# A graph message-passing kernel: X ahead of the prefix sums while no batch is in the pipe, and the aggregate's zeros copied by DMA

## The chip, the core and the metric

The kernel runs on one core of a Trainium2 chip. Its engines are TensorE (PE; PEld is its weight loading), VectorE (DVE), ScalarE (ACT), GpSimd (POOL) and SyncE (SP), which issues most DMAs. Each engine takes its own instructions in program order and waits on semaphores for the others. The metric is the device time of one execution in microseconds. Before the change it is 8952.63 us (median of 3 runs, 8952.41 to 8958.04).

## What is computed

N = 12500 nodes with D = 64 features, E = 800000 edges with 16 attributes each; `src` and `dst` are random.

```python
N, D = x.shape
m_in = jnp.concatenate([x[src], x[dst], e_attr], axis=-1)
msg = _silu(m_in @ w_msg)
agg = _segment_sum(msg, dst, N)
return _silu(jnp.concatenate([x, agg], axis=-1) @ w_upd)
```

## The kernel before

**Two pipes in one loop.** The edges arrive unsorted. The first pipe bins them by destination into 128 buckets of `BK = 98` nodes, in a DRAM store `st` that holds tiles of 128 records for each bucket. The second pipe takes full tiles out of the store, computes the messages of their edges and adds them to the aggregate `ACC`, which lies in SBUF as 128 partitions x 128 buckets x 98 nodes. One call of `period()` moves both pipes on by one stage. `step()` (L852) calls it 782 times with a new step of `M = 8` columns of 128 edges each; a batch of the second pipe comes along whenever a group of tiles is ready. Further calls after the steps work off what is left.

**The binning pipe.** Its stages are methods of `Step`, and their order over the engines is that of the calls in `period()` (L708), written out by hand. In period k, for the new step h = k, the step before it z = k-1, and the one before that p = k-2:

- `onehot` of h (L387): ACT writes the one-hots `hf` of the bucket numbers, eight squares (L391) and one Relu (L392).
- `count` of z (L411): PE makes in the PSUM tile `z`, of which there is one, the place of each edge in its bucket: from `hf` (L418), the running sums `G` (L419) and the last of these (L421).
- `ranks` of z (L423): DVE reduces `z` to one rank an edge (L426).
- `sums` of h (L394): the running sums `G` over four columns at a time, one copy on ACT (L398) and, for the first 140 steps, three additions on DVE (two of L400, one of L402). The count of the following period reads them.
- `expand` of z (L428): DVE writes the records into the slots that the ranks name, the rows `X`: L435, L436 and four multiplications of L439. There are two buffers of `X`. The move of the following period reads them.
- `move` of p (L442): 16 matmuls of `hf` and `X` (L456; one instruction of the program's eight is two in the profile) gather the records by bucket in the PSUM tile `pl`; ACT copies it to `blk` (L461).
- `place` (L470): DVE advances the buckets' pointers (L474, L475). POOL scatters `blk` to the store one period later (L479).

Records are made of the edge attributes `ea`, loaded by SP for three steps at a time (L243) and copied by ACT (L272).

**The message pipe.** A group of tiles is formed over several periods (`fourth`, L527): pointers on DVE, then a work list, then SP loads the tiles, 16 a period at first, from the store into one of four buffers `RT` (L561), and DVE takes the node numbers out of them (`sidx`, L522). A group's batches then run through `gather` (POOL, L642), `onehot` (L652, L653), `transpose`, `product`, `message`, `reduce` and `add` (L703), one period apart: in `period()` the names q, t, a and r are the new batch and those of one, two and three periods before. The first group needs as many records as fill its tiles, so the first 26 periods (0 to 25) have no batch. Periods 34 to 38 get no new batch either; the last ones before them are still under way in 34 and 35.

**Tables.** Beside the first steps, `tables()` (L211) makes from the node features x the products with the two halves of w_msg, four bucket rows an iteration: PE transposes and multiplies (L193, L198), ACT copies (L194, L204, L205), SP stores one product to DRAM (`A_d`, L209) and loads x for a later iteration (L187). `BW`, on chip, keeps the other and gets 16 rows of w_msg by one DMA of 512 KB (L352). After each of the steps 0 to 3 come four iterations, after each later one a single one, up to step 21.

**Zeros.** `later()` (L345) is called after each step from step 1 on, behind the step's tables, while its list lasts. It zeroes the four buffers `RT` (1088 columns of 128 partitions each) and `ACC` in four pieces (3136 columns each), all by ACT (L347). Behind the first piece SP writes sentinel tiles to the store, behind the third it issues the DMA into `BW`. A group may load fewer tiles than `RT` holds; the rest of the buffer keeps what is there.

Of the kernel before, what the change touches and what calls it, by code (L numbers as in the profile page):

```python
# [6 lines left out]
AF = mybir.ActivationFunctionType  # L7
# [8 lines left out]
NBK = 128  # L16
BK = 98
D = 64
DE = 16
R = DE + 1  # L20
# [12 lines left out]
GT = NBG * BT  # L33
# [15 lines left out]
def mpnn_kernel(tc, x, e_attr, src, dst, w_msg, w_upd, out):  # L49
    nc = tc.nc  # L50
# [22 lines left out]
    with es:  # L73
# [68 lines left out]
        done0 = cp.tile([NBK, 1], F32, name="done0")  # L142
# [190 lines left out]
        RT = [lp.tile([P, GT, R], F32, name=f"rt{i}") for i in range(4)]  # L333
        ACC = lp.tile([2 * D, NBK, BK], F32, name="ACC")
        ACCf = ACC.rearrange("p b k -> p (b k)")
# [3 lines left out]
        nc.gpsimd.memset(sent[:, :, DE:R], (P - 1) / 256.0)  # L339
        nc.gpsimd.memset(done0, 0.0)  # L340

        ZP = NBK // 4
        zeros = [RT[i].rearrange("p a c -> p (a c)") for i in range(len(RT))] + [ACC[:, b:b + ZP, :].rearrange("p b k -> p (b k)") for b in range(0, NBK, ZP)]

        def later():  # L345
            z = zeros.pop(0)
            nc.scalar.activation(z, done0[0:z.shape[0], :].to_broadcast(z.shape), AF.Copy)  # L347
            if len(zeros) == 7:
                for k in range(P // SR):
                    nc.sync.dma_start(st_t[D0:D0 + DUM, k * SR * R:(k + 1) * SR * R], sent[0:DUM].rearrange("p a b -> p (a b)"))  # L350
            elif len(zeros) == 5:
                nc.sync.dma_start(BW[BK:KQ], w_msg[2 * D:2 * D + DE, None, :].to_broadcast([DE, NBK, D]))  # L352


# [353 lines left out]
        def period(step=None, batch=None, ptr_new=None):  # L708

            h, z, p, s = step, pipe["h"], pipe["z"], pipe["s"]  # L710
            q, t, a, r = batch, pipe["q"], pipe["t"], pipe["a"]
            forms = [g for g in work["forming"] if not g.ready()]
            e = None
            pipe.update(h=h, z=z, q=q, t=t, a=a)
            if q:
                q.gather(0, BT // 2)
            if s:
                s.scatter()
            if q:
                q.gather(BT // 2, BT)  # L720
            if h:
                h.onehot()
            if q:
                q.onehot()
            for g in forms:
                g.fourth()
            if z:
                z.count()
            if t:
                t.transpose(0)  # L730
                t.weights()
                t.transpose(1)
            if r:
                r.reduce()
            if z:
                z.ranks()
            if a:
                a.message()
            if r:
                r.add()  # L740
            if h:
                h.sums()
            if z:
                z.expand()
            if p:
                e = p.move(0)
            if t:
                t.product()
            if p:
                p.move(1)  # L750
            if e:
                e.place(ptr_new)
            for g in forms:
                g.middle()
                g.fifth()
            pipe["s"] = e
            return r
# [4 lines left out]
        class Draws:  # L762
# [34 lines left out]
            def take(d, u, units):  # L797
                for f, done in zip(d.free(u), d.done):
                    left = units
                    for b in range(NB):  # L800
                        n = min(f[b], left)
                        done[b] += n
                        left -= n
# [48 lines left out]
        def step():  # L852
            c = None
            if flow["ic"] < len(steps):
                c = next_step(flow["ic"])
                flow["ic"] += 1
            pn = None
            if pipe["z"] and pipe["z"].last:
                if flow["npl"] % 64 == 0:
                    flow["ptrs"] = sg.tile([NBK, 64], I32, name="ptrs")  # L860
                pn = flow["ptrs"][:, flow["npl"] % 64:flow["npl"] % 64 + 1]
                flow["npl"] += 1
            b = take()
            if size() and may_start() and draws.holds(state["u"], size() // state["u"]):
                draws.take(state["u"], size() // state["u"])
                g = stages[state["stage"]]
                start_group(state["u"], state["ptr"], size(), cap=g["cap"], bt=g["bt"])
            elif not size() and (not work["forming"] or work["forming"][-1].k >= 2):
                larger_from()
            if pipe["z"]:  # L870
                for i in pipe["z"].last.values():
                    draws.place(Chunk(i).m)
            period(c, b, pn)
# [4 lines left out]
        while flow["ic"] < len(steps) or pipe["h"] or pipe["z"]:  # L878
            step()
            for _ in range(4 if flow["ic"] < 5 else 1):  # L880
                next(tab, None)
            if zeros and flow["ic"] > 1:
                later()
        while zeros:
            later()
# [23 lines left out]
        while pipe["s"]:  # L909
            period(None, take())  # L910
# [21 lines left out]
        while work["used"] < large or (work["forming"] and work["forming"][-1].k < 2):  # L932
            b = take()
            if work["used"] < large and may_start():
                start_group(QU, ptrg)
            period(None, b)
            next(upd, None)
            next(upd, None)
# [61 lines left out]
        while work["used"] < whole or lasts or work["cur"] is not None or work["forming"]:  # L1000
            b = take()
# [47 lines left out]
        with tc.If(more > 0):  # L1049
# [4 lines left out]
            with tc.If(nover > 0):  # L1054
# [27 lines left out]
                with tc.For_i(0, nover, 1):  # L1082
# [36 lines left out]
                    def block(rs=None):  # L1119
                        for c in halves:  # L1120
                            c.expand(rs)
                            e = c.move()
                        return e


                    c = block()
# [4 lines left out]
                    with tc.For_i(0, rounds, 1):  # L1131
                        c = block(rs)
# [36 lines left out]
```

## Time and profile before

One profiled execution; the "mean" of a group in the profile is the mean duration of one instruction.

| what | value |
|---|---|
| median of 3 runs | 8952.63 us |
| profiled execution, time | 8968.66 us |
| profiled execution, span from first to last instruction | 8966.8 us |
| PE busy | 8230.5 us (92%) |
| DVE busy | 7221.8 us (81%) |
| POOL busy | 6615.6 us (74%) |
| ACT busy | 5079.7 us (57%) |
| mean granted TensorE clock | 0.940 |
| first period with a batch, sidx of its group | 225.37 us |

How to read the rows: in the timeline a row starts with its start and its length in us, then the engine, the line, the operation and the tiles written and read; "x16" merges sixteen such instructions that follow one another, and the brackets at the end hold the idle time of the engine before them and who ended it. "SPq" is the DMA issue on SP. In the table of stages the columns are the stretch, its length, the busy us of PE, PEld, DVE, ACT and POOL with the count of instructions, the granted clock, the share of time that the 16 DMA engines are busy, and GB/s. A row of a DMA queue has its packets, its MB and the time of its packets as a share of 16 engines' time. A busy engine can still be waiting for nothing but its own chain: the share of a stage tells only whether an engine is full.

### The profile page before, as it was taken

To read this page: it belongs to the slowest core of one execution; us is meant where nothing else is said; L and a number is where in the kernel's file an instruction comes from. 1 tells how busy PE (TensorE), PEld (TensorE's weight loads), DVE (VectorE), ACT (ScalarE), POOL (GpSimd) and SP (SyncE) were. 2 spreads that over 40 slices of the span, in tenths; PEclk is the share of its full clock that TensorE was granted. 3 is DMA by queue.
4 is the path that set the end of the run, shared out by engine and by line. 5 is a ranking of instruction groups with operands and counts; after the bars stand their busy time and mean duration, and the time that the engine had idled before them with its cause. 6 is when DMAs were issued, how large, how long until landed. Compare 5 with 4: busy or idle time off the path is not lost. (4 is left out here: it accounts for less than half of the span.)

```text
span 8966.8 us, 156158 instructions
## 1 busy us (share of the span) xinstructions
PE 8230.5 (92%) x49816; PEld 5882.3 (66%) x49816; DVE 7221.8 (81%) x15722; ACT 5079.7 (57%) x12601; POOL 6615.6 (74%) x6908
## 2 busy tenths in 40 slices
PE   8899999999999999999999999999999999999767
PEld 5677766666666666666666666666666666666656
DVE  7999998888888888888888888888888888887233
ACT  7666666555555555555555555555555555555222
POOL 1677777777777777777777777777777777777776
PEclk9999999999999999999999999999999999999566
DMA  3222222221222222222222221221222122221223
GB/s 67 56 60 61 61 62 57 52 55 51 56 53 54 53 55 55 52 57 52 55 52 56 56 53 51 55 58 50 57 52 55 52 56 56 52 57 49 59 48 51
DMA packets 660741, 493.05 MB, mean 55 GB/s; under 512 B 492743, under 2 KB 529671, under 8 KB 659911
## 3 DMA queue, kind: packets, MB, share of 16 engines
q0 software_dynamic: 238976, 349.72, 15.0%
q1 hardware_dynamic: 420615, 133.18, 6.9%
q8 instruction: 401, 6.57, 0.3%
q14 instruction: 429, 3.51, 0.1%
q10 hardware_dynamic: 320, 0.07, 0.0%
HBM read 330.05 MB, written 152.30 MB: 54 GB/s over the span
## 5 line engine op out<-in xcount | busy, mean ns | idle before, releaser
L642 POOL DMA_INDIRECT g<-A_d,sidx x6322 | 6036.2, 955 | 1949.3 <-issue 1511.9
L456 PE MATMUL pl<-X,hf 128*128 128x291 f32 (+5 forms) x12512 | 4273.7, 494 | 35.8 <-DVE LOST L474 35.8
L456 PEld LDWEIGHTS pl<-X,hf 128*128 128x128 f32 x12512 | 2398.5, 198 | 1374.1 <-issue 883.0
L439 DVE TENSOR_TENSOR X<-cb,rec 128x442 f32<-128x442 f32 (+5 forms) x3128 | 2647.7, 909 | 26.7
L391 ACT ACTIVATE hf<-iof,shi 128x128 f32<-128x128 f32 x6256 | 1914.0, 392 | 892.7 <-PE pl L456 892.6
L670 PEld LDWEIGHTS pre<-w,qt 114*128 114x128 f32 x10496 | 1334.3, 202 | 585.0 <-issue 568.5
L670 PE MATMUL pre<-w,qt 114*128 114x64 f32 x10496 | 1338.1, 284 | 256.9 <-DVE g L674 255.4
L674 DVE TENSOR_TENSOR g<-pre,g 128x512 f32<-128x512 f32 (+1 forms) x818 | 549.2, 671 | 1191.5 <-DMA g<-A_d,sidx 764.5
L675 ACT ACTIVATE g<-g 128x512 f32<-128x512 f32 (+1 forms) x818 | 503.0, 615 | 1742.6 <-DVE g L674 1740.7
L691 PE MATMUL ag<-q,g 128*64 128x98 f32 x12644 | 775.0, 264 | 248.2 <-DVE wl L546 133.6
L426 DVE TENSOR_REDUCE rank<-z 128x8 f32<-128x1024 f32 x782 | 950.3, 1215 | 53.6 <-PE z L421 27.0
L392 ACT ACTIVATE hf<-hf,ones 128x1024 f32<-128x1024 f32 x782 | 900.4, 1151 | 25.4
L664 ACT ACTIVATE qt<-tq 114x1024 f32<-114x1024 f32 (+1 forms) x818 | 799.0, 977 | 158.7 <-PE tq L661 157.4
L661 PE MATMUL tq<-ident,q 128*114 128x128 f32 x6322 | 873.2, 283 | 14.4 <-ACT nodes L194 12.7
L691 PEld LDWEIGHTS ag<-q,g 128*64 128x64 f32 x12644 | 613.5, 143 | 410.3 <-issue 211.9
L661 PEld LDWEIGHTS tq<-ident,q 128*114 128x114 f32 x6322 | 768.6, 140 | 137.4 <-ACT nodes L194 20.1
L479 POOL DMA_INDIRECT st<-blk,ptrs x567 | 572.8, 1010 | 342.2 <-issue 145.7
L461 ACT ACTIVATE blk<-pl 128x512 f32<-128x512 f32 (+1 forms) x568 | 324.2, 571 | 798.1 <-PE pl L456 643.9
L652 DVE TENSOR_TENSOR q<-cb,lo 128x784 f32<-128x784 f32 (+1 forms) x818 | 768.4, 939 | 2.2
L418 PE MATMUL z<-hf,w 128*128 128x512 bf16 x1564 | 619.7, 396 | 3.2 <-ACT hf L392 3.2
L703 DVE TENSOR_TENSOR ACC<-ag,ACC 64x98 f32 x1938 | 498.0, 257 | 107.7 <-PE ag L691 29.3
L419 PE MATMUL z<-G,onesb 128*128 128x384 bf16 x1564 | 512.0, 327 | 3.0 <-DVE G L400 2.9
(138 smaller groups left out, 5123.2 us busy)
## 6 DMA issues: line engine op xcount, KB each, us to landing
g<-A_d,sidx POOLq DMA_INDIRECT x6322
ea<-in_e_attr SPq DMA_DIRECT2D x260, 192.0 KB
rt<-st SPq DMA_DIRECT2D x1312, 34.0 KB
st<-blk,ptrs POOLq DMA_INDIRECT x567
rt<-st SPq DMA_DIRECT2D x434, 8.5 KB
nodes<-in_x SPq DMA_DIRECT2D x62, 98.0 KB
rt<-st SPq DMA_DIRECT2D x320, 17.0 KB
A_d<-nodes SPq DMA_DIRECT2D x32, 98.0 KB
```

What stands on the lines that cost most here:

```text
L391: nc.scalar.activation(c.hf[:, k, :], iof, AF.Square, bias=c.hi[:, k:k + 1])
L392: nc.scalar.activation(c.hf, c.hf, AF.Relu, bias=ones, scale=-1.0)
L418: nc.tensor.matmul(c.z[:, k:k + ZB, :], w1, hb[:, k:k + ZB, :], start=True, stop=False)
L426: nc.vector.tensor_reduce(out=c.rank, in_=c.z, axis=AX.X, op=OP.max)
L439: nc.vector.tensor_tensor(out=c.x[:, k:k + 2, 2:2 + n * R].rearrange("p k (s c) -> p k s c", c=R), in0=hit[:, k:k + 2, 0:n, None].to_broad ...
L456: nc.tensor.matmul(pl[:, 0:w], c.hf[:, k, :], c.x[:, k, 0:w], start=(n == (c.size - 1 if whole else 0)), stop=ends, skip_group_check=True)
L642: j = nc.gpsimd.indirect_dma_start(out=t.g[:, i, :], out_offset=None, in_=A_d, in_offset=bass.IndirectOffsetOnAxis(ap=t.grp.sidx[:, k:k + ...
L652: nc.vector.tensor_tensor(out=t.q[:, 0:n, 0:BK], in0=ioB[:, None, 0:BK].to_broadcast([P, n, BK]), in1=t.grp.lo[:, i0:i0 + n, None].to_broa ...
L661: nc.tensor.transpose(t.tq[0:KQ, j * P:(j + 1) * P], t.q[:, j, :], ident)
L664: nc.scalar.activation(t.qt[:, 0:w], t.tq[0:KQ, 0:w], AF.Copy)
L670: nc.tensor.matmul(t.pre[:, i * D:(i + 1) * D], t.qt[:, i * P:(i + 1) * P], w, start=True, stop=True)
L691: o = nc.tensor.matmul(t.ag[t.half(v), v // 2 * BK:(v // 2 + 1) * BK], t.g[:, i, :], t.q[:, i, 0:BK], start=(k == 0), stop=(k == u - 1))
```

## The change

In `period()` the prefix sums of h come behind the rows X of z, but only in periods in which no batch of the stages q, t or a is in the pipe; otherwise the order stays. In `later()` the list is cut finer: `ACC` in pieces of 1088 columns (eleven, and a last one of 576) instead of 3136, so 16 pieces in all instead of eight. Only the first, `RT[0]`, is zeroed by ACT; the other fifteen are copied by SP's DMA from `RT[0]`. The sentinel tiles and the DMA into `BW` stay behind the first and the third piece.

```diff
-        ZP = NBK // 4
-        zeros = [RT[i].rearrange("p a c -> p (a c)") for i in range(len(RT))] + [ACC[:, b:b + ZP, :].rearrange("p b k -> p (b k)") for b in range(0, NBK, ZP)]
+        ZP = GT * R
+        zeros = [RT[i].rearrange("p a c -> p (a c)") for i in range(len(RT))] + [ACCf[:, b:min(b + ZP, NBK * BK)] for b in range(0, NBK * BK, ZP)]
 
         def later():
             z = zeros.pop(0)
-            nc.scalar.activation(z, done0[0:z.shape[0], :].to_broadcast(z.shape), AF.Copy)
-            if len(zeros) == 7:
+            if len(zeros) == 15:
+                nc.scalar.activation(z, done0[0:z.shape[0], :].to_broadcast(z.shape), AF.Copy)
+            else:
+                nc.sync.dma_start(z, RT[0].rearrange("p a c -> p (a c)")[:, 0:z.shape[1]])
+            if len(zeros) == 15:
                 for k in range(P // SR):
                     nc.sync.dma_start(st_t[D0:D0 + DUM, k * SR * R:(k + 1) * SR * R], sent[0:DUM].rearrange("p a b -> p (a b)"))
-            elif len(zeros) == 5:
+            elif len(zeros) == 13:
                 nc.sync.dma_start(BW[BK:KQ], w_msg[2 * D:2 * D + DE, None, :].to_broadcast([DE, NBK, D]))
...
                 a.message()
             if r:
                 r.add()
-            if h:
+            early = q or t or a
+            if h and early:
                 h.sums()
             if z:
                 z.expand()
+            if h and not early:
+                h.sums()
             if p:
                 e = p.move(0)
```

## The prediction

> **What bounds the kernel now.** I read the page first, for where idle time sits; then the table of stages, because the change touches only periods without a batch; then the groups, the timeline and the queues of that stretch alone. A "period" is one call of `period()`; period k builds the one-hots of step k, counts and ranks step k-1, and moves step k-2.
>
> Table of stages: length, then busy time of each engine with its instruction count, then the granted clock, DMA share and GB/s.
>
> ```profile
> 26.00:63.60 37.60, 34.48 (x148) 22.74 (x146) 24.28 (x49) 31.42 (x82) 4.04 (x4) 0.95 0.58 110
> 63.60:192.80 129.20, 109.66 (x434) 69.68 (x433) 99.26 (x219) 97.83 (x237) 15.57 (x17) 0.95 0.23 58
> 440.00:8300.00 7860.00, 7388.06 (x44962) 5206.83 (x44960) 6644.49 (x14257) 4630.53 (x11576) 5965.24 (x6214) 0.97 0.21 55
> ```
>
> In the long stage (440 to 8300 us) TensorE is busy 94%, and a batch is always in the pipe there: the new order doesn't apply, and the zeroing is long over. From 63.6 to 192.8 us no batch exists and no engine is full (PE 85%, DVE 77%, ACT 76%): that stage is bound by a chain that hops between engines. The groups of the first 200 us name it (busy, mean ns, then idle time before and who ended it), and the rank row of 63 to 193.5 us counts its periods:
>
> ```profile
> L456 PE MATMUL pl<-X,hf 128*128 128x410 f32 (+3 forms) x339 | 102.7, 458 | 20.6 <-DVE LOST L474 20.6
> L400 DVE TENSOR_TENSOR G<-hf 128x256 bf16<-128x256 f32 x23 | 9.8, 425 | 42.4 <-ACT hf L392 42.4
> L347 ACT ACTIVATE ACC<-done 128x3136 f32<-128x3136 f32 x4 | 11.3, 2827 | 0.0
> L347 ACT ACTIVATE rt<-done 128x1088 f32<-128x1088 f32 x4 | 4.4, 1111 | 0.0
> ...
> L426 DVE TENSOR_REDUCE rank<-z x17: 1202/1219/1225, 63.6 to 192.8; 128x8 f32<-128x1024 f32 x17
> ```
>
> DVE idles 42.4 us in front of the prefix sums, for ACT's one-hots; behind the sums it then writes X, and PE idles 20.6 us for X (the release is put on L474, DVE's next instruction after X). Sixteen periods take 129.2 us, 8.07 us each. One pass of the chain, from the timeline:
>
> ```profile
> 102.39 0.39 PE L418 MATMUL z<-hf,w 128*128 128x512 bf16 x1
> 103.16 0.38 PE L421 MATMUL z<-G,onesb 128*128 128x512 bf16 x1
> 103.38 4.48 PE L456 MATMUL pl<-X,hf 128*128 128x410 f32 x16
> 103.58 1.23 DVE L426 TENSOR_REDUCE rank<-z 128x8 f32<-128x1024 f32 x1 [1.04 <-PE z L421]
> 107.86 1.03 PE L198 MATMUL abp<-wab,nodes 128*98 128x256 f32 x4
> 108.73 0.39 PE L418 MATMUL z<-hf,w 128*128 128x512 bf16 x1
> 109.21 0.38 ACT L205 ACTIVATE BW<-abp 98x256 f32<-98x256 f32 x1
> 109.89 2.44 ACT L391 ACTIVATE hf<-iof,shi 128x128 f32<-128x128 f32 x8
> 113.54 0.43 DVE L400 TENSOR_TENSOR G<-hf 128x256 bf16<-128x256 f32 x1 [0.55 <-ACT hf L392]
> 114.67 0.16 DVE L435 TENSOR_TENSOR X<-rank,limc 128x8 f32<-128x8 f32 x1
> 115.19 3.01 DVE L439 TENSOR_TENSOR X<-cb,rec 128x442 f32<-128x442 f32 x4
> 118.34 4.55 PE L456 MATMUL pl<-X,hf 128*128 128x410 f32 x16 [0.18 <-DVE LOST L474]
> ```
>
> Move (103.38), tables, ACT's copies of them (to 109.59), one-hots (from 109.89; the sums start behind them at 113.54), sums (to 114.67), X (to 118.20), move (118.34): 14.96 us for two periods, **7.48 us a period**. The zeros of L347 stand on ACT between the copies and the one-hots, on this chain: that is how 7.48 became 8.07 and more. The clock adds to it:
>
> ```profile
> 55.53 6.06 PE L456 MATMUL pl<-X,hf 128*128 128x410 f32 x16 [2.71 <-DVE LOST L474]
> 94.44 7.08 PE L456 MATMUL pl<-X,hf 128*128 128x410 f32 x16 [2.92 <-DVE LOST L474]
> 349.69 4.56 PE L456 MATMUL pl<-X,hf 128*128 128x410 f32 x16 [2.05 <-DVE LOST L474]
> ```
>
> After idling 2.7 to 2.9 us the same move takes 6.1 to 7.1 us; after 2.05 us it takes 4.56.
>
> **The change, part by part.**
>
> *X ahead of the sums.* ACT's order does not change (expand issues nothing there, so L398 keeps its place), nor PE's. On DVE the three additions of the sums (113.54 to 114.67, 1.13 us) go behind X (114.67 to 118.20, 3.53 us). X needs only the rank, so it no longer waits for the one-hots, and the 7.48 chain is cut: one-hots now reach PE through sums and count alone, which leaves out the 3.53 us of X in two periods, (14.96 - 3.53) / 2 = 5.7 us. What waits instead: the next count needs the sums, and they now end last. New loop: rank 1.22, X 3.53, sums to end of count, then rank again. The last piece shows where a count waited for the sums:
>
> ```profile
> 89.63 0.43 DVE L400 TENSOR_TENSOR G<-hf 128x256 bf16<-128x256 f32 x1 [5.10 <-ACT hf L392]
> ...
> 90.58 0.34 PE L419 MATMUL z<-G,onesb 128*128 128x384 bf16 x1 [0.54 <-DVE G L400]
> ...
> 91.14 0.38 PE L421 MATMUL z<-G,onesb 128*128 128x512 bf16 x1
> ```
>
> 89.63 to 91.52 is 1.89, and a rank follows its count by 0.04 (103.54 to 103.58). Loop: 1.22 + 3.53 + 1.89 + 0.04 = **6.7 us**. PE's own work is 102.39 to 108.73 without a gap, 6.34 us, so PE idles about 0.35 us a period, far under the 2.05 that left the clock alone. Bounds of the period: 6.34 (PE alone) and 7.48 (the order gives nothing). I take 6.7, since each piece has a row.
>
> *The zeros.* ACT loses seven of eight writes: 3 x 1.11 + 4 x 2.83 = 14.6 us. Two of them (after periods 2 and 3, with four tables each) I count at nothing: PE covers them, as the first row shows.
>
> ```profile
> 32.00:42.00 10.00, 9.81 (x45) 6.57 (x46) 6.24 (x13) 8.89 (x25) 1.15 (x1) 1.00 0.52 118
> ...
> q0 software_dynamic: 238976, 349.72, 15.0%
> ...
> q1 hardware_dynamic: 12079, 3.95, 13.0%
> q0 software_dynamic: 1024, 3.34, 9.2%
> ...
> SPq L209 <- ACT nodes L204: 105.5, 16, 10.9
> ```
>
> Were that cover gone, they would be worth 2.2 us. In place of the seven come 15 copies of 128 x 4352 B = 557 kB (the last 295 kB), after periods 2 to 16, on SP's queue. SP waits 105.5 us in the first 230 us for ACT's copies (last row), so issuing 15 more costs nothing. What one copy occupies, T, no row shows. The page's q0 (second row) moved 349.72 MB in 15.0% of 16 engines x 8966.8 us: 260 GB/s, T = 2.1. q1 between 60 and 190 us moved 3.95 MB in 13.0%: 234 GB/s, T = 2.4. The slow end is the 512 KB into BW with the 192 KB edge load behind it, from 46.41 to 54.03 us:
>
> ```profile
> 46.41 0.43 SPq L352 DMA_DIRECT2D BW<-in_w_msg  x1
> 46.90 1.15 SPq L243 DMA_DIRECT2D ea<-in_e_attr  x1
> ...
> 54.03 0.53 ACT L272 ACTIVATE rec<-ea 128x384 f32<-128x384 f32 x1 [0.51 <-DMA ea<-in_e_attr]
> ...
> 58.10 0.43 DVE L400 TENSOR_TENSOR G<-hf 128x256 bf16<-128x256 f32 x1 [1.18 <-ACT hf L392]
> ```
>
> 721 kB in 7.62 us is 95 GB/s, T = 5.9. I take 2.3: whole rows of 4352 B are nearer to q0's big packets than to BW's small ones.
>
> One copy is on the path: that after period 3 is issued just ahead of BW, and ACT already waits for the edge load behind both. The landing goes from 54.03 to 56.3; sums follow 4.07 us later (58.10 - 54.03), at 60.4, and the rank 1.89 + 0.04 later, at 62.3, where it was at 63.6 before. From there 16 periods of 6.7 are 107.2. DVE also has the work list of the first group in periods 20 and 21, about 0.85 us each; between sums and rank there are 0.8 us of slack, of which the pointers take 0.4, so 0.5 us sticks out each time, 1.0 in all.
>
> 62.3 + 107.2 + 1.0 = 170.5, against 192.84 before: **22.3 us earlier**.
>
> *What it meets there.* Right before that rank, SP is given the first group's rows:
>
> ```profile
> 192.84 1.20 DVE L426 TENSOR_REDUCE rank<-z 128x8 f32<-128x1024 f32 x1
> 204.25 19.59 SPq L561 DMA_DIRECT2D rt<-st  x32
> ...
> 225.37 0.21 DVE L522 CAST sidx<-rt 128x64 int32<-128x64 f32 x1 [5.39 <-DMA rt<-st]
> ```
>
> Its 48 loads are paced by SP at 0.6 us each, and the first batch waits for the last. So periods 22 to 25 gain nothing, but the whole row of loads starts 22.3 us earlier, and so does everything behind it. Those loads overwrite the buffer that the copies read; the last copy is issued some 40 us before, so the wait is free (2.3 us if not). The aggregate's first addition comes later still.
>
> Periods 36 to 38, between two groups, are the only others without a batch:
>
> ```profile
> 335.90 1.22 DVE L426 TENSOR_REDUCE rank<-z 128x8 f32<-128x1024 f32 x1
> ...
> 342.89 1.22 DVE L426 TENSOR_REDUCE rank<-z 128x8 f32<-128x1024 f32 x1
> ```
>
> 6.99 us there against 6.7, and period 36 has additions ahead of X: between -1 and +1 us, taken as 0.
>
> *The sum.* The profiled run took 8968.66 us (span 8966.8); less 22.3 it is 8946.4. It lies 16 us above the median of the runs, 8952.63, and nothing in these stages explains that, so I take the same 22.3 off the median: **8930 us**.
>
> *Two rules set beside this.* Period 5 would leave PE idle for about 2.4 us, between the 2.05 and 2.71 of the rows. The Trainium skill (TensorE: Matmul & The Clock Gate, "Part 1: The HAM clock gate") has the clock halve after an idle window of about 3.4 us; by that the move stays at 4.5 us and the sum at 8930. The trace had slow moves after 2.7 us already, so the page's figure is too long for these rows; with a slow move it is up to 8932. The Trainium skill (DMA: Bandwidth & Descriptors, "Anatomy of one DMA") gives about 2.0 us plus bytes over 436 GB/s, an estimate of 3.3 us for a copy, and says under "Issuing engines are not separate DMA queues" that all transfers share 16 engines, which speaks against putting zeros there; by it the edge load lands 1.0 us later and the sum is 8931.
>
> **The rivals.**
>
> *PE becomes the bound.* If the handoffs of the loop overlap more than the rows say, the period is 6.34 and the 1.0 of the work list vanishes: 5.8 + 1.0 more, 8924. For it: the two lengths are only 0.36 us apart. Against: rank, X and sums are all on one engine, in order.
>
> *The order gives nothing, only the zeros leave.* If the late sums hold the count as long as X held the move, the period stays 7.48: 16 x 0.78 = 12.5 us less, 8943. For it: 6.99 us between ranks in the old order at 336 us, where there are no tables.
>
> *Slower: the copies fill the DMA engines.* Other traffic takes 13.0% on q1 and 9.2% on q0 (the rows of 60 to 190 us) of the 8.07 us, about 1.8 us a period. Once T + 1.8 passes 6.7, loads for the next steps queue up behind zeros in the same queue, and 13 periods (4 to 16) run at the copies' pace. The gain is then 22.3 - (T - 2.3) - 13 (T - 4.9) = 88.3 - 14 T: nothing is left at T = 6.3, and at T = 8 it is 24 us slower, 8976. For it: BW's 95 GB/s (T = 5.9) is just short of that point. Against: both queues' means are 2.5 times as fast.
>
> *It is taken back at the first batch*, should the loads there wait for something that doesn't move (scattered blocks, the issue of SP): about 8948.
>
> **How the numbers follow.** Forecast 0.56, PE bound 0.14, order without effect 0.16, slower 0.08, taken back 0.06. The forecast's own range, with periods of 6.4 to 7.0, is 8925 to 8936. The range goes on to the PE bound with 3 us less waiting in period 5 on one side and to the order without effect on the other, 8919 to 8944; outside it lie the slower case, taken back, and some edges. A measurement of this kernel tells about 0.2% (18 us) from no change, so the border is 8934.7: faster 0.68 (forecast without its upper edge, and PE bound), same 0.24, slower 0.08.
>
> **What would show it.** Right: about 6.7 us between ranks from 62 to 170 us, the idle time in front of L400 gone and a short one in front of L419 for G in its place, moves of 4.5 us throughout, the sidx of the first group near 203 us, copies of 2 to 3 us. Wrong: periods of 7.4 (the order), copies of over 5 us with L272 or L193 waiting for DMA (the queue), or a first batch that comes less early than the ranks before it.

## The result, and the profile after

The changed kernel takes 8932.38 us (median of 13 runs), against 8952.41 us for the kernel before in the same comparison: ratio 0.9978 [0.997, 0.9986], 20.0 us less. One of the 13 runs took 17042.83 us at a granted clock of 0.514; it does not enter the ratio, and the other twelve lie between 8928.93 and 8936.42 us.

The profiled execution of the changed kernel took 8929.85 us, with a span of 8928.0. The kernel before's had a span of 8966.8, so the two profiles lie 38.8 us apart, not 20. At the first batch they are 22.4 us apart (below); the rest grows evenly, by some 0.03 us a period, through the long stage, where nothing was changed. It is about the 16 us by which before's profiled execution lay above its own median (the changed kernel's lay 2.5 us under its own), so it is taken for scatter and not for a part of the result.

The stages, with the columns of the prediction (stretch, length, busy time of PE, PEld, DVE, ACT and POOL with their counts, granted clock, DMA share, GB/s), and below them the row that counts the ranks (shortest, median and longest in ns; first and last start):

```profile
25.80:63.20 37.40, 33.28 (x143) 21.88 (x144) 24.46 (x50) 28.70 (x82) 4.03 (x4) 0.96 0.77 172
63.20:170.80 107.60, 103.43 (x425) 67.71 (x433) 100.25 (x220) 86.61 (x230) 16.00 (x17) 1.00 0.41 124
170.80:203.00 32.20, 26.25 (x101) 16.72 (x100) 25.01 (x55) 15.78 (x38) 2.87 (x3) 1.00 0.25 41
440.00:8261.00 7821.00, 7298.62 (x44064) 5181.04 (x44792) 6616.00 (x14193) 4603.53 (x11537) 5933.19 (x6195) 0.97 0.23 55
```

```profile
L429 DVE TENSOR_REDUCE rank<-z x17: 1215/1224/1226, 63.2 to 170.8; 128x8 f32<-128x1024 f32 x17
```

The second stage is the one to read: the same sixteen periods took 129.2 us before and take 107.6 us now, 6.73 us each. PE's work in it is nearly the same instruction count (425 for 434), but its share rose from 85% to 96% (103.43 of 107.60), DVE's from 77% to 93%, and the clock from 0.95 to 1.00. The first stage ends only 0.4 us earlier, so nearly all of the gain is made between 63 and 171 us. The long stage has PE at 93%, where it had 94%.

The groups of the first 200 us show where the idle time went:

```profile
L459 PE MATMUL pl<-X,hf 128*128 128x410 f32 (+3 forms) x393 | 110.9, 435 | 0.0
L429 DVE TENSOR_REDUCE rank<-z 128x8 f32<-128x1024 f32 x25 | 30.6, 1223 | 22.6 <-PE z L424 22.5
L422 PE MATMUL z<-G,onesb 128*128 128x384 bf16 x52 | 17.5, 336 | 9.8 <-DVE G L403 7.7 <-issue 0.2
L403 DVE TENSOR_TENSOR G<-hf 128x256 bf16<-128x256 f32 x26 | 10.9, 417 | 7.1 <-ACT hf L395 7.1
```

The 20.6 us in which PE idled for X before the move are 0.0. The 42.4 us in which DVE idled for the one-hots before the sums are 7.1. In their place stands a short wait on each side of the new loop: PE waits for the sums in front of the count (7.7 us), DVE for the count in front of the rank. One period in full, from the timeline:

```profile
96.74 1.23 DVE L429 TENSOR_REDUCE rank<-z 128x8 f32<-128x1024 f32 x1 [0.27 <-PE z L424]
98.00 0.17 DVE L438 TENSOR_TENSOR X<-rank,limc 128x8 f32<-128x8 f32 x1
98.53 3.01 DVE L442 TENSOR_TENSOR X<-cb,rec 128x442 f32<-128x442 f32 x4
101.45 0.41 DVE L403 TENSOR_TENSOR G<-hf 128x256 bf16<-128x256 f32 x1
102.94 0.38 PE L424 MATMUL z<-G,onesb 128*128 128x512 bf16 x1
103.16 4.48 PE L459 MATMUL pl<-X,hf 128*128 128x410 f32 x16
103.36 1.22 DVE L429 TENSOR_REDUCE rank<-z 128x8 f32<-128x1024 f32 x1 [0.38 <-PE z L424]
```

Rank, X, sums and count follow one another without a gap on DVE but the last (0.38 us, for the end of the count), and from rank to rank it is 6.62 us. The first batch then comes as early as the ranks before it; in the kernel before its sidx started at 225.37 us:

```profile
171.53 9.12 SPq L564 DMA_DIRECT2D rt<-st  x16
...
182.36 18.88 SPq L564 DMA_DIRECT2D rt<-st  x32
...
202.93 0.22 DVE L525 CAST sidx<-rt 128x64 int32<-128x64 f32 x1 [5.71 <-DMA rt<-st]
```

### The profile page after: what moved, and what is told of

The parts are those of the page before. It is cut to its first block, busy times and chain, and to the rows that moved or that the text cites. A ratio compares the mean times of both kernels' runs of the same rounds, so it can differ in the third digit from the quotient of the medians.

```text
span 8928.0 us, 155380 instructions
## 1 busy us (share of the span) xinstructions
PE 8156.2 (91%) x49053; PEld 5873.2 (66%) x49816; DVE 7216.6 (81%) x15722; ACT 5054.3 (57%) x12594; POOL 6599.6 (74%) x6908
## 3 DMA queue, kind: packets, MB, share of 16 engines
q0 software_dynamic: 238976, 349.72, 16.8%
## 5 line engine op out<-in xcount | busy, mean ns | idle before, releaser
L664 PE MATMUL tq<-ident,q 128*114 128x128 f32 x6322 | 871.5, 283 | 14.3 <-ACT nodes L194 13.0
L664 PEld LDWEIGHTS tq<-ident,q 128*114 128x114 f32 x6322 | 766.9, 140 | 136.5 <-ACT nodes L194 20.5
L673 PE MATMUL pre<-BW,qt 114*128 (+1 forms) x2148 | 311.8, 305 | 109.4 <-DVE g L677 108.6
```

The lines of the kernel that those rows point to most:

```text
L664: nc.tensor.transpose(t.tq[0:KQ, j * P:(j + 1) * P], t.q[:, j, :], ident)
L673: nc.tensor.matmul(t.pre[:, i * D:(i + 1) * D], t.qt[:, i * P:(i + 1) * P], w, start=True, stop=True)
```

## Experiments

The forecast takes the two parts of the change together and gives no split. The rivals left were that the order gives nothing and only the zeros leave, and that the copies nearly fill the DMA engines, so that a somewhat slower copy would undo everything. For the first four kernels the kernel before took 8952.94 us (median of 31 runs).

### The copies alone

The changed kernel with the old order in all periods:

```diff
-            early = q or t or a
-            if h and early:
+            if h:
                 h.sums()
             if z:
                 z.expand()
-            if h and not early:
-                h.sums()
```

> The changed kernel with the order of before in every period: only the zeros are copied by DMA. My theory: the chain move, tables, one-hots, sums, X (7.48 us a period) still binds, so the ranks of periods 6 to 22 stand 7.5 us apart, the edge load of period 5 lands 2.4 us later than before, and the gain is 7 to 10 us: 8943 to 8945 us. Rival (the zeros alone carry the gain, the order gives nothing): 8932 us, ranks 6.7 us apart.

8948.77 us, ratio 0.9995 [0.9986, 1.0004]: 4.2 us less, where 7 to 10 were expected, and the interval does not tell it from no change. The row of the ranks, the wait of ACT and the timeline around the first rank of that row show what moved:

```profile
L429 DVE TENSOR_REDUCE rank<-z x17: 1202/1218/1225, 67.0 to 186.6; 128x8 f32<-128x1024 f32 x17
```

```profile
ACT rec L272 <- DMA ea<-in_e_attr: 5.1, 1, 5.1
```

```profile
58.02 0.52 ACT L272 ACTIVATE rec<-ea 128x384 f32<-128x384 f32 x1 [5.11 <-DMA ea<-in_e_attr]
...
66.89 6.02 PE L459 MATMUL pl<-X,hf 128*128 128x410 f32 x16 [2.19 <-DVE LOST L477]
...
219.07 0.21 DVE L525 CAST sidx<-rt 128x64 int32<-128x64 f32 x1 [5.39 <-DMA rt<-st]
```

Sixteen periods take 119.6 us, 7.48 each on average: that is the chain of 14.96 us for two periods that was added up from before's timeline, though single pairs of periods take from 13.8 to 16.9 us. So the copies do take 0.6 us a period off ACT's path, 9.6 us in all. But 3.4 us of it are lost before: the first rank of the row is at 67.0 instead of 63.6, because ACT waits 5.1 us for the edge attributes, which stand in SP's queue behind a copy and the DMA into BW. (0.6 of the 3.4 is there at the second rank of the execution already, at 27.1 us here, at 26.5 in before and at 25.8 in after. Differences of 1 us between single profiles are no more than that.)

### The order alone

The kernel before, with the block on `early` of the diff and nothing else; all zeros stay on ACT.

> The kernel before with the new order alone; ACT writes all the zeros as before. My theory: with the 7.48 us chain cut, a period is bound by DVE's loop (6.7 us) except in the four periods in which ACT writes a piece of the aggregate (5.6 us of own work plus 2.8, about 8.6 us instead of 10.0); the edge load of period 5 lands as before. Gain 3.6 (first rank) + 5.6 + 7.8 = 17 us: 8935 us. So the two parts add up to more than the whole (17 + 8 against 20), since both shorten one chain. Rival (the order needs the zeros gone to do anything): 8945 us or more.

8933.73 us, ratio 0.9979 [0.997, 0.9988]: 19.2 us less, 17 expected.

```profile
L426 DVE TENSOR_REDUCE rank<-z x17: 1215/1224/1226, 59.8 to 172.2; 128x8 f32<-128x1024 f32 x17
```

```profile
204.36 0.21 DVE L522 CAST sidx<-rt 128x64 int32<-128x64 f32 x1 [5.74 <-DMA rt<-st]
```

The first rank comes 3.4 us before that of the whole change, since nothing stands in front of BW; the four periods with a piece of ACC then take 7.7 to 8.4 us, and the last rank is 1.4 us behind the whole change. The medians differ by the same 1.4 us (8933.73 and 8932.38), which by themselves they could not tell.

### The DMA into BW moved behind the copies

In the changed kernel, with `len(zeros)` 0 the DMA into BW comes behind the last copy, far from any load that ACT needs in period 5.

```diff
-            elif len(zeros) == 13:
+            elif len(zeros) == 0:
```

> The changed kernel with the 512 KB DMA into BW issued behind the last zero copy instead of behind the third piece. My theory: the edge load of period 5 no longer stands behind BW in the queue, ACT does not wait 4.8 us for it, the ranks of periods 5 and 6 stand 6.7 us apart instead of 10.9, and everything behind comes 4.2 us earlier: 8928 us. Rival (the zero copies and tables hold the edge load): no change, 8932 us.

8928.87 us, ratio 0.9975 [0.9965, 0.9985], 3.5 us under the changed kernel; the two intervals overlap, so the medians alone do not tell the two apart.

```profile
L429 DVE TENSOR_REDUCE rank<-z x17: 1215/1224/1226, 60.1 to 167.6; 128x8 f32<-128x1024 f32 x17
```

```profile
52.80 0.53 ACT L272 ACTIVATE rec<-ea 128x384 f32<-128x384 f32 x1
...
200.16 0.21 DVE L525 CAST sidx<-rt 128x64 int32<-128x64 f32 x1 [6.06 <-DMA rt<-st]
```

ACT's copy of the edge attributes no longer waits, the ranks come 3.1 us earlier than after's (4.4 counted from the second rank of each execution, which is at 27.1 here and 25.8 there; the spans differ by 4.3), and the periods are the same 6.72 us. In these ranks the copies cost nothing but this one collision in period 5.

### The copies in small pieces

Fourteen of the copies made of pieces of 68 bytes, one record each, which makes them slow. Their source changes with it: each reads the first record of `RT[0]` 64 times.

```diff
-                nc.sync.dma_start(z, RT[0].rearrange("p a c -> p (a c)")[:, 0:z.shape[1]])
+                if zeros:
+                    nc.sync.dma_start(z.rearrange("p (a c) -> p a c", c=R), RT[0][:, 0:1, :].to_broadcast([P, GT, R]))
+                else:
+                    nc.sync.dma_start(z, RT[0].rearrange("p a c -> p (a c)")[:, 0:z.shape[1]])
```

> The changed kernel with 14 of the 15 zero copies cut into pieces of 68 B (each reads one row of 17 zeros 64 times), 8192 packets a copy instead of 128. At the 12 ns that a 68 B packet takes in the trace, a copy holds the 16 DMA engines for 6.1 us instead of 1.4. Theory 1 (my formula for the slower rival, loads wait in the same queue): 88.3 - 14 x 6.1 = 3 us are left of the gain, 8949 us, with ACT or PE waiting for DMA loads in many periods. Theory 2 (the loads are issued so far ahead that the backlog is hidden): only period 5 waits longer, by 4.7 us: 8937 us.

8952.12 us, ratio 1.0 [0.9991, 1.0009]. The gain of 20 us is gone. The queue from 60 to 150 us (packets, MB, share of 16 engines), the waits and the ranks:

```profile
q1 hardware_dynamic: 102823, 9.75, 114.4%
```

```profile
ACT rec L272 <- DMA ea<-in_e_attr: 20.8, 5, 7.5
```

```profile
L432 DVE TENSOR_REDUCE rank<-z x17: 1216/1224/1225, 72.5 to 191.9; 128x8 f32<-128x1024 f32 x17
```

Nearly the same bytes take the queue's full time (a share above 100% counts packets that overlap). ACT waits for edge attributes five times, 20.8 us, and the rank of period 22 is at 191.9, 0.9 us before that of the kernel before. The slower rival's formula, 88.3 - 14 T, gave 3 us left at T = 6.1: the total is right to 2 us. Its split is not. It had every one of 13 periods pay; what was paid is 9.3 us ahead of the first rank of the row and 12 us behind it, most of them in every third period (9.8, 10.3 and 9.3 us long), when new edge attributes are due. On average the kernel does run at about the copies' pace: twelve periods from 72.47 to 163.71 us, 7.6 us each, where T + 1.8 is 7.9. That the total agrees so well with another split is in part luck.

### The order in all periods, and the rest

For the remaining eight runs the kernel before itself took 11055.3, 10827.64 or 11085.5 us; the record has these runs on other chips (5, 0 and 4) than the first four kernels (13). In the traces of the eight the ranks up to the first batch come as above, but the long stage takes some 13 us a period instead of 11. Waits stand in it for a releaser that the profile calls "remote" (2475.3 us of ACT's in front of L664 in the second run of the order with BW late), of which the changed kernel's trace has none. The cause was not found; so only ratios within one comparison are used, and none of these runs says what the kernel would do where before takes 8952 us.

Without the condition, the sums come behind X in all periods, with a batch in the pipe too:

```diff
-            early = q or t or a
-            if h and early:
-                h.sums()
             if z:
                 z.expand()
-            if h and not early:
+            if h:
                 h.sums()
```

> The changed kernel with the sums behind X in every period, with or without a batch. My theory: in the long stage PE is busy 94% and counts first in each period; in a timeline of it X and its neighbours end only 0.5 us after the next count has begun, so sums put behind X reach the count 0.1 to 0.3 us late in most of 750 periods: 75 to 220 us slower than the changed kernel, 9010 to 9150 us, with PE waiting in front of L419's counterpart for G. Rival (DVE has slack there, the condition is not needed): 8932 us, within 0.2%.

> The same kernel as e5, sums behind X in every period, again: in the first run of it the kernel before took 11055 us with PE waiting for other things in the long stage, so it could not tell how the order stands where PE is busy 94% there. With the kernel before near 8953 us, my theory as before: PE waits for G in most periods of the long stage, 75 to 220 us slower than the changed kernel, 9010 to 9150 us. Rival (slack, or X earlier is of use there too): 8932 us or less.

> Sums behind X in every period, a third time; the two runs so far stand where the kernel before took 11055 and 10828 us, and gave ratios of 0.994 and 1.000. In the second the ranks fell 60 us behind the conditional order in the first 150 steps and came back 30 us in the rest. With the kernel before near 8953 us my theory, lowered by that: PE waits for G 0.1 us a period in the first 140 steps (chunks of eight) and about nothing later, 8945 to 9010 us. Rival: the later steps give more than the first ones take, under 8932 us.

Ratios 0.994 [0.9927, 0.9953], 1.0001 [0.9992, 1.001] and 0.9953 [0.9937, 0.9969]: a miss in all three. The first two were expected 75 to 220 us above the changed kernel, which is 0.6% or more above before, and fit neither that nor their rivals; the third was expected between level with before and 0.6% above it, and fits its rival (under 8932 us). In the second comparison the cost that was expected can be seen, in PE's waits from 3000 to 6000 us (total, count, longest):

```profile
PE z L422 <- DVE G L403: 166.3, 122, 3.8
```

PE waited for the late sums in 122 of its counts there. The same window has no such wait in the kernel of that comparison that keeps the condition (the next one below), nor in the changed kernel, whose largest are:

```profile
PE pre L673 <- DVE g L677: 100.7, 57, 3.1
PE ag L694 <- DVE wl L549: 48.5, 27, 3.8
```

So the wait that the condition avoids does arise. What it costs is seen against the kernel that keeps the condition: level with it at the rank of step 21, the order in all periods is 64 us behind at step 150 and, from there on, gains: 32 us behind at the last rank. In the first comparison it is 12 us behind at step 150 and 45 us ahead at the last rank. In these single profiles it loses in the first 140 steps and gains later. How much of the gain is due to the order is not shown: in the third comparison two kernels that are alike from step 140 on (the last one below, and this one) drift 29 us apart between step 150 and the last rank. By the medians the order in all periods is 48 us faster than the kernel with the condition in the first comparison and 19 us slower in the second. Whether the condition is needed where before takes 8952 us stays open.

The kernel before with the order alone and its DMA into BW behind the last piece of zeros (`len(zeros) == 5` to `0`, and the block on `early`), which asks whether the late BW is worth anything where no copies stand in front of it:

> The kernel before with the new order, ACT's zeros, and the DMA into BW moved behind the last zero. It asks what copying the zeros by DMA is worth once the edge load is not in the way. My theory: the order alone did not wait for the edge load, so moving BW gives nothing here: 8933 to 8934 us, and the zeros by DMA with BW late (8928.9) are worth 4 to 5 us, from the four periods of 7.8 to 8.2 us in which ACT writes the aggregate's pieces. Rival (BW late gives the same 3.5 us without the copies): 8930 us.

> The same kernel as e6 (order, ACT's zeros, BW late) again, for a run in which the kernel before takes near 8953 us. My theory: 8933 to 8934 us, so that copying the zeros by DMA is worth 4 to 5 us once BW is late (8928.9 with both). Rival: 8930 us.

Ratios 0.9985 [0.9976, 0.9994] and 0.9981 [0.9972, 0.999]; the first is 9.1 us and the second 18.7, about the 19.2 us of the order alone. In the trace of the second, period 5 takes 6.62 us, where it took 7.23 with the order alone. More than that the late BW is not shown to give by itself, and the times near 8930 us that were expected cannot be checked here.

The late BW and, for the first groups, every second eight of the tile loads issued by ACT instead of SP, since the first batch waits for SP's issue:

```diff
+                        act = g.u == 1 and g.cap is not None and u // 8 % 2
-                        for i, t in enumerate(regs(g.row, u, min(8, gu - u), ENG.SP, TOP - g.u)):
-                            j = nc.sync.dma_start(
+                        for i, t in enumerate(regs(g.row, u, min(8, gu - u), ENG.Activation if act else ENG.SP, TOP - g.u)):
+                            j = (nc.scalar if act else nc.sync).dma_start(
...
```

> The changed kernel with BW late, and half of the first groups' tile loads (every second eight of them) issued by ACT instead of SP. It asks what the 22 us meet at the first batch. My theory: SP's pace of 0.6 us a load sets the first sidx; with half of the loads gone it would be ready 14 us earlier, but ACT pays 4.8 us in each of the periods 22 to 24, which then take 8.7 us, so that the first batch comes at about 199 us as before: 8928 to 8930 us. Rival (ACT has the room): periods 22 to 25 stay at 6.7 us, the first batch comes at 193 to 194 us and the time is 8924 us.

> The same kernel as e7 (BW late, half of the first groups' loads issued by ACT) again, for a run in which the kernel before takes near 8953 us. The trace of the first run has periods 22 to 24 of 8.0 to 8.5 us and the first sidx at 197.6 us, where the kernel with BW late alone would have it at about 199: so 8927 to 8929 us, no change that can be told. Rival: 8924 us.

Ratios 0.9967 [0.9955, 0.998] and 0.9973 [0.9963, 0.9982]. From the timeline of the second:

```profile
168.41 4.34 SPq L565 DMA_DIRECT2D rt<-st  x8
168.82 5.08 ACTq L565 DMA_DIRECT2D rt<-st  x8
...
175.38 1.22 DVE L429 TENSOR_REDUCE rank<-z 128x8 f32<-128x1024 f32 x1
...
184.39 1.23 DVE L429 TENSOR_REDUCE rank<-z 128x8 f32<-128x1024 f32 x1 [0.87 <-PE z L422]
```

Issuing eight loads holds ACT for 5.08 us, and the periods there grow from 6.6 to 7.7 and 9.0 us, since ACT also has the one-hots. The first sidx comes at 198.5 us, 1.7 us before that of the late BW without this, so ACT loses most of what SP saves, as was expected. The late BW without it had 0.9975 in its comparison, so a gain in time is not shown.

The last one has the late BW, and the sums ahead of X only where a batch is in the pipe and the step is one of the first 140 (`turn` is 3 there); from then on X comes first always:

```diff
-            early = q or t or a
+            early = (q or t or a) and h and h.turn == 3
```

> The changed kernel with BW late and the sums behind X not only without a batch but in every period from step 140 on (chunks of twelve). Theory, from the second run of the order everywhere (30 us regained in steps 150 to 781): 5 to 30 us below the kernel with BW late alone (ratio to before 0.9973 to 0.998): ratio 0.994 to 0.997. Rival (PE is the bound and only waits more for G): ratio above 0.998, slower than with the condition.

Ratio 0.994 [0.9924, 0.9956], where 0.994 to 0.997 was expected. The order in all periods has 0.9953 [0.9937, 0.9969] in the same comparison and had 0.994 in the first, so the two are not told apart, and this one was not run where before takes 8952 us. At step 150 it is 22 us ahead of the order in all periods (4 of them since period 6, by the late BW), as the loss in the first 140 steps says; at the last rank it is 7 us behind, though from step 140 on the two have the same order, which nothing here explains.

## Why the prediction was right

**The new loop.** 6.7 us were added up from four rows of before (rank 1.22, X 3.53, sums to the end of the count 1.89, 0.04). The plain period is 6.62, 96.74 to 103.36; four of the sixteen are about 0.4 us longer, two of them (7.07 and 7.00) at the periods of the work list, where 0.5 each was set. All sixteen take 107.6 us, where 6.7 x 16 + 1.0 = 108.2 was set. The PE-bound rival (6.34) falls: with PE busy 96%, PE still waits 7.7 us for the sums and DVE for the count. That the old order would stay at 7.48 with the zeros gone was right on average (the copies alone), and the rival in which the new order gives nothing falls with the order alone, 19.2 us.

**Period 5.** The landing of the edge attributes was set at 56.3 and the rank at 62.3; they came at 56.47 and 63.20. From the timeline of after:

```profile
46.03 0.49 SPq L350 DMA_DIRECT2D rt<-rt  x1
...
46.97 0.33 SPq L355 DMA_DIRECT2D BW<-in_w_msg  x1
...
47.36 2.92 SPq L243 DMA_DIRECT2D ea<-in_e_attr  x1
...
56.47 0.53 ACT L272 ACTIVATE rec<-ea 128x384 f32<-128x384 f32 x1 [4.83 <-DMA ea<-in_e_attr]
...
60.55 0.42 DVE L403 TENSOR_TENSOR G<-hf 128x256 bf16<-128x256 f32 x1 [3.50 <-ACT hf L395]
60.56 0.58 PE L421 MATMUL z<-hf,w 128*128 128x512 bf16 x1 [3.00 <-ACT hf L395]
...
62.95 4.89 PE L459 MATMUL pl<-X,hf 128*128 128x410 f32 x16
63.20 1.22 DVE L429 TENSOR_REDUCE rank<-z 128x8 f32<-128x1024 f32 x1 [1.11 <-PE z L424]
```

From landing to sums it is 4.08 (4.07 predicted), from sums to rank 2.65 where 1.93 was set. These 0.7 us are the clock: the granted clock is 0.50 from 60.4 to 63.7 us, and the count's matmuls take 0.58 instead of 0.39. The sum had left it at full speed; it cost 0.4 us on the move (4.89 for 4.48) and 0.7 on the count.

The prediction judged the clock by the idle stretch just ahead of a move: slow after 2.7 us, not after 2.05. The rows of the granted clock (third from the end) do not bear that out. Two of before, and one of the copies alone:

```profile
92.00:93.00 1.00, 0.00 (x0) 0.00 (x0) 1.00 (x2) 1.00 (x1) 0.00 (x0) 0.85 0.78 209
93.00:94.00 1.00, 0.00 (x0) 0.00 (x0) 1.00 (x2) 1.00 (x2) 0.00 (x0) 0.50 0.96 259
```

```profile
65.00:66.00 1.00, 0.00 (x0) 0.00 (x0) 1.00 (x3) 0.98 (x4) 0.00 (x0) 0.50 0.97 254
```

In before the clock halved at 92.7 us, 1.2 us into the idle stretch that ended with the slow move at 94.44. With the copies alone it halved at 63.0 us, in the middle of a count, so the 2.19 us of idling ahead of the slow move at 66.89 came after it. Read in steps of 0.1 us, the slow spells last 3.4 us (55.1 to 58.5 in before, 60.4 to 63.7 here) or twice that (92.7 to 99.5 in before, 63.0 to 69.8 with the copies alone). The Trainium skill (TensorE: Matmul & The Clock Gate, "Part 1: The HAM clock gate") has the clock halve after an idle window of about 3.4 us, and says that this window is free-running; the length of the spells in these traces agrees with that figure. Ahead of these spells and in them PE idled for 3.00 us at the most in one stretch, so a window with little work in it was enough. The prediction's remark that this figure is too long takes the window for an idle stretch.

**T, the term that was mis-sized.** 2.3 us was taken from the mean rates of the queues, and copies of 2 to 3 us were to be a sign of being right. From 60 to 150 us the copies can be measured against before; first after, then before:

```profile
q1 hardware_dynamic: 12322, 9.37, 33.4%
...
ACC<-rt SPq DMA_DIRECT2D x10, 544.0 KB
```

```profile
q1 hardware_dynamic: 9721, 3.05, 14.6%
```

6.32 MB more take 18.8% more of 16 engines x 90 us, 271 engine-us: 373 GB/s over all 16, so T = 557 kB / 373 GB/s = 1.5 us. (Some of the extra bytes are loads that come sooner.) The mean rates had come from other packets: 1463 B is the mean of those in q0 (349.72 MB in 238976), a third of a row of the copies. By the Trainium skill (DMA: Bandwidth & Descriptors, "Where 436 GB/s comes from") the ceiling of 435 GB/s would make it an estimate of 1.3 us, which the trace nearly reaches. The 3.3 us that the prediction set beside its own figure are a sum that the Trainium skill (DMA: Bandwidth & Descriptors, "Anatomy of one DMA") gives for DMAs issued by GpSimd; the copies are issued by SP.

The landing came out right all the same, and that is luck: the copy was set 0.8 us too long, and the step had a second part, which the prediction put at nothing (issuing 15 more costs nothing). BW itself is issued 0.56 us later (46.97 for 46.41, behind the copy's issue of 0.49 us). The remaining 1.9 us are put down to the copy ahead of it; that is 0.4 us more than T, and no run separates the two.

**Who gains what.** The prediction gave no split; the runs do. All times of one profiled execution each in us, but the medians:

| kernel | rank of period 6 | of period 22 | first sidx | median | gain at sidx | gain of the median |
|---|---|---|---|---|---|---|
| before | 63.6 | 192.8 | 225.4 | 8952.9 | | |
| copies alone | 67.0 | 186.6 | 219.1 | 8948.8 | 6.3 | 4.2 |
| order alone | 59.8 | 172.2 | 204.4 | 8933.7 | 21.0 | 19.2 |
| after | 63.2 | 170.8 | 202.9 | 8932.4 | 22.4 | 20.0 |
| after, BW late | 60.1 | 167.6 | 200.2 | 8928.9 | 25.2 | 24.1 |
| after, small pieces | 72.5 | 191.9 | 224.0 | 8952.1 | 1.4 | 0.8 |

The order is nearly all of it: by itself it brings the rank of period 22 forward by 20.6 us, and on top of the copies by 15.8 (186.6 to 170.8). The two parts overlap, since both shorten one chain. With the order alone the four periods with zeros of ACC take 31.7 us (ranks from 59.82 to 91.50) where the same four take 26.9 in after (63.20 to 90.12); the copies save these 4.8 us, lose 3.4 in period 5, and 1.4 are left. The last column counts from the median of before in each kernel's own comparison, 8952.41 for after and 8952.94 for the others.

**What follows the first batch.** 22.3 us were to be kept, and the rank of period 22 came 22.0 and the sidx 22.4 us earlier (202.93, predicted near 203). Two small errors nearly cancel in it: the rank of period 6 came 0.9 us later than set, and the sixteen periods took 0.6 us less. The 48 loads pace periods 22 to 25 as before, so the rival "taken back" falls. In every kernel the gain of the median is 0.6 to 2.4 us under the one at the sidx. All these gains are counted from one profile of before, so they are not independent. Whether the difference is given back later or is the scatter of single profiles, about 1 us at their second rank already, stays open; it is the size by which the forecast of 8930 was off.

**The slower rival** needed another T: with 6.1 us the copies in small pieces undid the gain, within 2 us of its sum though not by its split, and the 1.5 us of the real copies is far from its border of 6.3.

## What to carry to other kernels

Where every engine is below 90%, add up one pass of the chain from the timeline, cut it where an instruction only stands in line, and add up the loop that closes next: this gave the new period within 0.1 us, and it was the order of two steps on one engine, not an amount of work, that by itself was worth 19.2 us where the whole change gave 20.0. Work moved to an idle engine's queue is free only at its own place in it: look for the load behind it that another engine waits for, and move what is slow (here the DMA into BW, 3.1 us at the ranks) away from it. Look at the length of the pieces of a copy between on-chip buffers: here rows of 4352 B were hidden in all places but one, and pieces of 68 B, read from one record, cost the whole gain.

## What the runs showed of the hardware

- A 557 kB copy from one on-chip buffer to another in rows of 4352 B occupied the 16 DMA engines for about 1.5 us; cut in pieces of 68 B, read from one repeated record, the same bytes filled the queue (114.4% of 16 engines between 60 and 150 us).
- The granted clock of TensorE fell to 0.50 for 3.4 or 6.8 us at a time, though PE idled for 3.00 us at the most in one stretch, once 1.2 us into an idle stretch and once in the middle of a count. Moves in such a spell took 6.02 to 7.08 us instead of 4.48.
- ACT spent 5.08 us on issuing eight DMAs, 0.6 us each, which is SP's price too (18.88 us for 32).
